# Block-causal attention feeding two mixture layers on one core: small two-operand VectorE steps turned into one-operand steps or handed to GpSimd, and the background squares tied to a place in ScalarE's queue

## The chip, the core and the metric

The program runs on one core of a Trainium2 chip. The metric is the device time of one execution in microseconds (us). The kernel before took 702.68 us as the median of three runs (700.4 to 709.11 us). Five engines work side by side: TensorE (PE, with its weight loads listed as PEld), VectorE (DVE), ScalarE (ACT), GpSimd (POOL) and the queue of SyncE (SP), which here only issues DMAs. Each engine takes its own instructions in the order fixed when the program was built, and waits at the head of its queue for what the instruction needs.

## What is computed

```
attention: 8 batches x 8 heads, 576 positions, head size 64, fp32
  scores = q k^T / 8, causal in blocks of 64 positions
  x = softmax(scores) v        -> 4608 tokens x 512
soft mixture: logits = x @ phi (32 slots)
  d = softmax over tokens, slot_in = d^T x, 8 experts (relu(slot_in w1) w2)
  c = softmax over slots, x = c @ slot_out
gated layer: (x w1) * (x w2) @ w3 @ w_out
```

The weights come as 64-bit floats and are narrowed to 32 bits on the chip with integer steps.

## The kernel before

The work goes in **pairs of heads**: 32 pairs, four to a batch. For a pair, PE computes raw scores only to find a row maximum per 64-block (`max_tile`, L177, seven tiles, each followed by a VectorE reduction into `bm`, L191 or L196). `level2` (L212) adds a mask to `bm`, once for each of five window lengths (L218, 250 elements per partition), and reduces to the row maxima `m` (L220). `mrow` (L223) turns `m` into rows through PE (L231, L234) that ScalarE copies into the operand set of the pair (L235). `qk_unit` (L241) then computes the scores again, transposed and with maximum and mask folded in, and ScalarE takes the exponentials into `PTa` (L263) and `PTb` (L271). `preadd` (L273) is GpSimd's: it adds pieces of the exponentials for the row sums (L287). `pv` (L297) multiplies by v, with the last 64 keys on half of the array's rows (L319). `sums` (L324) makes the row sums (L333). `prep_lo` (L148) splits the operands of a later pair on GpSimd (L153), and SP moves the parts into place (L174).

After each batch a **tail** of 18 steps (`push_tail`, L346) computes slot logits, the combine weights (`combine` to `combine3`, L394 to L407), the running maximum and sum of the dispatch softmax (`disp_max`, L432 to L458) and the sum over tokens (`slot_in`, L468, whose last 64 tokens use half the array's rows, L473). Its steps are spread over the following four pairs. The order inside a pair is one string, `ORDER` (L524), where M is a max tile, Q a score unit, T a tail step, L2 `level2`, MR `mrow`, A `preadd`, SU `sums`, V `pv`, PH and PL the operand preparation, LD the loads of the next operands.

BG in `ORDER` is one **background** turn: a DMA loads a piece of a weight of the last layer (L637) and `narrow` (L613) converts it: three integer steps on VectorE (L623, L624, L625), a square on ScalarE (L627) that marks values to be flushed, and a select on VectorE (L631). There are 16 pieces, spread over the pairs; one buffer holds the raw piece. `issue_after(ins)` puts an instruction behind `ins` in the queue of `ins`'s engine and binds no other engine: before, a turn's VectorE steps stand behind the `level2` of pair n+1 (L593), and its square on ScalarE is free. The program order is a priority only; a planner with a simulated timeline fixes each engine's order from it.

The later stage (`Rest.run`, L657 and `final`, L949) computes the experts and the last layer after the attention; the change does not touch it, but for the weights that the background turns have narrowed.

Of the kernel before, what the change touches and what calls it, by code (L numbers as in the profile page):

```python
# [54 lines left out]
class Attn:  # L55


    def __init__(self, tc, ctx, io, nb, keep, after_scores=None, background=()):
# [19 lines left out]
        self.bm, self.m, self.PT, self.acc, self.l2 = {}, {}, {}, {}, {}  # L78
# [4 lines left out]
        self.lmask = self.const.tile([128, 5, 2, 25], F32, name="lmask")  # L83
# [24 lines left out]
    def constants2(self):  # L108
# [7 lines left out]
        nc.gpsimd.memset(self.dT[:, S:SP], 0.0)  # L116

# [59 lines left out]
    def max_tile(self, n, i):  # L177
# [3 lines left out]
        if n not in self.bm:  # L181
            self.bm[n] = self.st_p.tile([128, 2, 25], F32, tag="bm", name="bm")
        bm, R1, T1 = self.bm[n], self.R1b[n % NB], self.T1b[n % NB]
# [9 lines left out]
        if i == 6:  # L193
            mm(0, 0, 4, 320, 256)
            mm(256, 1, 4, 576, 256)
            nc.vector.tensor_reduce(bm[:, :, 21:25], ps.rearrange("p (h n k) -> p h n k", h=2, k=64), axis=AX.X, op=ALU.max)  # L196
            return
        h, w = divmod(i, 3)
        k0 = KB[h]
        if w == 0:  # L200
            mm(0, h, 3, k0, 448)
            mm(448, h, 0, k0, 64)
            red(bm[:, h, 0:8], 512)
        elif w == 1:
            mm(0, h, 2, k0, 320)
            mm(320, h, 1, k0, 192)
            red(bm[:, h, 8:16], 512)
        else:
            mm(0, h, 4, k0 + 192 * h, 320)
            red(bm[:, h, 16:21], 320)  # L210

    def level2(self, n):  # L212
        if n not in self.bm or n >= self.n_pairs:
            return
        nc = self.nc
        bm = self.bm.pop(n)
        t = self.st_p.tile([128, 5, 2, 25], F32, tag="l2", name="l2")
        nc.vector.tensor_tensor(t, bm.unsqueeze(1).to_broadcast([128, 5, 2, 25]), self.lmask, op=ALU.add)  # L218
        m = self.st_p.tile([128, 5, 2], F32R, tag="m", name="m")
        self.l2[n] = nc.vector.tensor_reduce(m, t, axis=AX.X, op=ALU.max).ins  # L220
        self.m[n] = m

    def mrow(self, n):  # L223
# [7 lines left out]
        nc.tensor.matmul(a[0:2, 0:64], lhsT=m[:, 0, :], rhs=self.negI[:, 0:64], start=True, stop=True)  # L231
        for c in range(1, 5):
            o = a[0:2, 128 * c - 64:128 * c + 64] if c < 4 else b[0:2, 0:128]
            nc.tensor.matmul(o, lhsT=m[:, c, :], rhs=self.negI, start=True, stop=True)  # L234
# [6 lines left out]
    def qk_unit(self, n, h, u):  # L241
# [22 lines left out]
        else:  # L264
# [6 lines left out]
            nc.scalar.activation(out=PTb[:, S * h:S * h + w], in_=ps[:, 256:256 + w], func=AF.Exp, scale=SCALE)  # L271
# [25 lines left out]
    def pv(self, n, part):  # L297
# [48 lines left out]
    def push_tail(self, b):  # L346
# [10 lines left out]
        st = {}  # L357

# [43 lines left out]
        def combine3():  # L402
# [4 lines left out]
            nc.vector.tensor_tensor(C, C, sm.unsqueeze(2).to_broadcast([128, 5, 32]), op=ALU.mult)  # L407
# [24 lines left out]
        def disp_max():  # L432
# [4 lines left out]
            M, old = self.keep["M"][b % 2], self.keep["M"][1 - b % 2]  # L437
            mm = tl([128, 2], "dmm")
# [7 lines left out]
            ac = tl([128, 2], "dac")  # L446
# [3 lines left out]
            if b:  # L450
                al = tl([128, 1], "dal")
                nc.scalar.activation(out=al, in_=old, func=AF.Exp, bias=ng)
                nc.vector.tensor_tensor(Ls, Ls, al, op=ALU.mult)
                nc.vector.tensor_tensor(Ls, Ls, ac[:, 0:1], op=ALU.add)
                st["al"] = al
            else:
                nc.vector.tensor_copy(Ls, ac[:, 0:1])
            nc.vector.tensor_tensor(Ls, Ls, ac[:, 1:2], op=ALU.add)  # L458
# [9 lines left out]
        def slot_in():  # L468
# [3 lines left out]
            for g in range(4):  # L472
                nc.tensor.matmul(ps[32 * g:32 * g + 32, 128 * g:128 * g + 128], lhsT=st["d"][0:64, 4, :], rhs=xT[0:64, g, 512:640], start=False, stop=True)  # L473
# [655 lines left out]
```

## Time and profile before

| | |
|---|---|
| median of the runs | 702.68 us |
| time of the profiled execution | 702.59 us |
| its span, first to last instruction | 700.8 us |
| mean granted TensorE clock | 0.966 of full |
| busy: PE / VectorE / ScalarE / GpSimd | 634.3 / 512.6 / 348.0 / 343.0 us |
| attention, about | 0 to 460 us |
| experts, last weights | 461 to 588 us |
| final products | 588 to 701 us |

The span is split into stretches by when the lines run. The busy time of PE counts modelled ends of pipelined matmuls, so that a busy PE is not PE at its peak. The granted clock of a stretch is a mean of two levels, 1.0 (2.4 GHz) and 0.5 (1.2 GHz). "Idle before, releaser" says what ended an engine's idle time.

### The profile page before, as it was taken

What the parts mean: (1) busy time and instruction counts of PE and PEld (TensorE: products, weight loads), DVE (VectorE), ACT (ScalarE), POOL (GpSimd) and SP (SyncE); (2) the same over time, 40 slices, a digit from 0 to 9 for tenths busy, and PEclk for the clock granted to TensorE, in tenths of its full rate; (3) what the DMA queues carried; (4) which work ended last, traced back from release to release, by engine and by line L of the source; (5) the groups of instructions that cost most, each with busy time, mean ns of one, the idle gap of its engine ahead of it and who ended that gap; (6) DMA issues with size and microseconds to landing.
All of it is one profiled execution on the core that took longest, in us unless ns stands there. A gap on an engine that the chain in (4) does not pass through costs nothing. (4 is left out here: it accounts for less than half of the span.)

```text
span 700.8 us, 11771 instructions
## 1 busy us (share of the span) xinstructions
PE 634.3 (91%) x4423; PEld 451.2 (64%) x4423; DVE 512.6 (73%) x877; ACT 348.0 (50%) x638; POOL 343.0 (49%) x266
## 2 busy tenths in 40 slices
PE   4779898989997979997999999777999998999997
PEld 2667675766675757565777775533665566888886
DVE  7778778878878778788689666699962699645460
ACT  6756554645654654564465553244442335444441
POOL 7747674754764656566467454033432432233220
PEclk9889999999999999998899999997999999999999
DMA  6588876676867566867476767999988112566642
GB/s 205 152 212 206 242 179 198 169 185 164 237 150 202 150 174 148 213 175 181 123 195 159 209 219 246 353 337 388 394 312 314 63 61 74 170 214 214 226 174 90
DMA packets 59640, 141.53 MB, mean 202 GB/s; under 512 B 5800, under 2 KB 23848, under 8 KB 59560
## 3 DMA queue, kind: packets, MB, share of 16 engines
q1 hardware_dynamic: 59404, 140.71, 67.3%
q8 instruction: 35, 0.57, 0.3%
q14 instruction: 21, 0.17, 0.1%
q10 hardware_dynamic: 180, 0.07, 0.0%
HBM read 96.52 MB, written 10.32 MB: 152 GB/s over the span
## 5 line engine op out<-in xcount | busy, mean ns | idle before, releaser
L254 PE MATMUL sc<-set 128*128 128x320 f32 (+4 forms) x704 | 134.9, 326 | 9.8 <-ACT PTb L271 8.9
L191 DVE TENSOR_REDUCE bm<-mx 128x8 f32<-128x512 f32 (+1 forms) x192 | 113.4, 616 | 18.0 <-PE mx L188 17.0
L254 PEld LDWEIGHTS sc<-set 128*128 128x128 f32 x704 | 103.7, 199 | 18.5 <-ACT PTb L271 11.3
L287 POOL TENSOR_TENSOR acc<-PTa 128x640 f32<-128x640 f32 x31 | 49.2, 1588 | 134.7 <-PE sum L333 134.7
L188 PE MATMUL mx<-set 128*128 128x320 f32 (+4 forms) x384 | 89.2, 336 | 22.8 <-DVE bm L191 15.5
L1014 PE MATMUL ops<-H,Ph 128*128 128x512 f32 x288 | 90.7, 395 | 3.3 <-ACT H L918 2.4
L188 PEld LDWEIGHTS mx<-set 128*128 128x128 f32 x384 | 66.8, 210 | 37.9 <-DVE bm L191 20.3
L153 POOL TENSOR_TENSOR set<-raw,set 128x1152 fp32r<-128x1152 f32 x29 | 76.7, 2644 | 19.1 <-ACT set L145 18.9
L321 ACT COPY xT<-pv 128x320 f32<-128x320 f32 x64 | 25.3, 399 | 115.8 <-PE pv L319 96.3
L314 PE MATMUL pv<-PTa,v 128*64 128x320 f32 (+2 forms) x512 | 71.6, 380 | 0.0
L989 POOL TENSOR_TENSOR Pl<-rot,Ph 128x384 fp32r<-128x384 f32 x24 | 30.3, 1282 | 75.8 <-ACT Ph L987 75.8
L287 POOL TENSOR_TENSOR acc<-acc,PTb 128x640 f32<-128x640 f32 (+1 forms) x62 | 65.7, 1059 | 2.7
L1014 PEld LDWEIGHTS ops<-H,Ph 128*128 128x128 f32 x288 | 54.3, 189 | 17.0 <-ACT H L918 2.9
L263 ACT ACTIVATE PTa<-sc 128x960 f32<-128x960 f32 x64 | 59.5, 976 | 0.5 <-PE sc L254 0.4
L1014 PE MATMUL ops<-H,Pl 128*128 128x512 f32 x144 | 56.9, 395 | 0.0
L710 PE MATMUL wps<-wo,w 128*128 128x512 f32 x192 | 51.4, 412 | 2.9 <-POOL wo L655 1.7
L314 PEld LDWEIGHTS pv<-PTa,v 128*64 128x64 f32 x512 | 34.5, 140 | 29.0 <-issue 6.4
L1017 ACT COPY o<-ops 128x512 f32<-128x512 f32 x36 | 21.1, 588 | 57.0 <-PE ops L1016 56.7
L710 PEld LDWEIGHTS wps<-wo,w 128*128 128x128 f32 x192 | 35.2, 192 | 20.4 <-issue 6.7
L271 ACT ACTIVATE PTb<-sc 128x704 f32<-128x704 f32 x64 | 44.0, 694 | 7.5 <-PE sc L254 7.5
L314 PE MATMUL pv<-PTb,v 128*64 128x320 f32 (+1 forms) x256 | 44.4, 420 | 0.0
L655 POOL TENSOR_TENSOR w<-f,w 128x512 fp32r<-128x512 f32 x16 | 20.6, 1294 | 30.1 <-ACT w L654 27.4
(203 smaller groups left out, 1196.1 us busy)
## 6 DMA issues: line engine op xcount, KB each, us to landing
set<-set SPq DMA_DIRECT2D x116, 288.0 KB, 3.2
win<-in_moe_w SPq DMA_DIRECT2D x16, 2048.0 KB
raw<-in_qk SPq DMA_DIRECT2D x31, 576.0 KB, 5.1
v<-in_v SPq DMA_DIRECT2D x32, 288.0 KB, 4.3
rot<-cs SPq DMA_DIRECT2D x48, 192.0 KB, 3.7
out<-o SPq DMA_DIRECT2D x11, 768.0 KB, 4.5
raw<-in_moe_w SPq DMA_DIRECT2D x16, 512.0 KB, 4.7
w3raw<-in_w3T SPq DMA_DIRECT2D x16, 512.0 KB, 12.3
```

The source lines that it names most:

```text
L153: nc.gpsimd.tensor_tensor(T1[:, 0:2 * S], self.raw.pop(n), flat(R1).bitcast(F32), op=ALU.subtract)
L188: nc.tensor.matmul(ps[:, o0:o0 + kn], lhsT=R1[:, h, q0:q0 + 128], rhs=T1[:, k0:k0 + kn], start=True, stop=True)
L191: red = lambda out, n: nc.vector.tensor_reduce(out, ps[:, 0:n].rearrange("p (n k) -> p n k", k=64), axis=AX.X, op=ALU.max)
L254: nc.tensor.matmul(ps[:, o0:o0 + qn * (qs.stop - qs.start)], lhsT=lt[:, k0:k0 + 128], rhs=rt[:, qs, q0:q0 + qn], start=st, stop=not st)
L263: nc.scalar.activation(out=PTa[:, h], in_=ps[:, 0:960], func=AF.Exp, scale=SCALE)
L271: nc.scalar.activation(out=PTb[:, S * h:S * h + w], in_=ps[:, 256:256 + w], func=AF.Exp, scale=SCALE)
L287: add = lambda o, a, b: eng.tensor_tensor(o, a, b, op=ALU.add)
L314: nc.tensor.matmul(ps[64 * h:64 * h + 64, q0 - lo:q1 - lo], lhsT=v[:, 128 * j + 64 * h:128 * j + 64 * h + 64], rhs=pt[:, h, o:o + q1 - q0] ...
L321: nc.scalar.copy(self.xTb[b % 2][:, p, lo:hi], ps[:, 0:hi - lo])
L710: nc.tensor.matmul(p, lhsT=a[:, o], rhs=b, start=c + i == 0, stop=c == 7 and i == 2)
L989: eng.tensor_tensor(Pl[:, k], p, Ph[:, k].bitcast(F32), op=ALU.subtract)
L1014: nc.tensor.matmul(ps, lhsT=a[:, k, r], rhs=b[:, k], start=n == 0, stop=False)
```

## The change

`level2` works on a new layout: `bm` holds five windows of nine places in two fixed, zeroed buffers, the mask is added once (90 elements per partition instead of 250), on GpSimd for all pairs but the first two, and VectorE reduces nine places at a time. In the tail, the subtraction and the product of the combine weights go to GpSimd (VectorE keeps them in the last batch). The running maximum and the running sum become one-operand reductions over three columns; the product for the sum goes to ScalarE. In `pv` and `slot_in` the half-row matmuls use all 128 rows, the other half being multiplied by zeros. The background turns are split: turn i narrows piece i and then issues the load of piece i+1, and whatever a turn issues on ScalarE stands behind the last exponential of the preceding pair.

```diff
+        self.bmb = [self.const.tile([128, 2, 45], F32, name=f"bm{i}") for i in range(2)]
+        for t in self.bmb:
+            nc.vector.memset(t, 0.0)
...
+        for t in self.xTb:
+            nc.gpsimd.memset(t[64:128, :, S:SP], 0.0)
...
-        nc.vector.tensor_tensor(t, bm.unsqueeze(1).to_broadcast([128, 5, 2, 25]), self.lmask, op=ALU.add)
-        m = self.st_p.tile([128, 5, 2], F32R, tag="m", name="m")
-        self.l2[n] = nc.vector.tensor_reduce(m, t, axis=AX.X, op=ALU.max).ins
+        t = self.st_p.tile([128, 2, 45], F32, tag="l2", name="l2")
+        (nc.vector if n < self.ML else nc.gpsimd).tensor_tensor(t, self.bmb[n % 2], self.lmask, op=ALU.add)
+        m = self.st_p.tile([128, 2, 5], F32R, tag="m", name="m")
+        self.l2[n] = nc.vector.tensor_reduce(m, t.rearrange("p h (w k) -> p h w k", k=9), axis=AX.X, op=ALU.max).ins
...
+            self.last_exp[n] = nc.scalar.activation(out=PTb[:, S * h:S * h + w], in_=ps[:, 256:256 + w], func=AF.Exp, scale=SCALE).ins
...
-                r = slice(64 * h, 64 * h + 64)
-                nc.tensor.matmul(ps[r, 256:320], lhsT=v[r, 512:576], rhs=PTb[r, 2 * S + 64 * h:2 * S + 64 * h + 64],
+                nc.tensor.matmul(ps[64 * h:64 * h + 64, 256:320], lhsT=v[:, 512:576], rhs=PTb[:, 2 * S + 64 * h:2 * S + 64 * h + 64],
                                  start=False, stop=True)
...
+        eng = nc.vector if b == self.nb - 1 else nc.gpsimd
-            nc.vector.tensor_tensor(C, L, mx.unsqueeze(2).to_broadcast([128, 5, 32]), op=ALU.subtract)
+            eng.tensor_tensor(C, L, mx.unsqueeze(2).to_broadcast([128, 5, 32]), op=ALU.subtract)
-            nc.vector.tensor_tensor(C, C, sm.unsqueeze(2).to_broadcast([128, 5, 32]), op=ALU.mult)
+            eng.tensor_tensor(C, C, sm.unsqueeze(2).to_broadcast([128, 5, 32]), op=ALU.mult)
...
-            if b:
-                nc.vector.tensor_tensor(mm[:, 0:1], mm[:, 0:1], old, op=ALU.max)
-            nc.vector.tensor_tensor(M, mm[:, 0:1], mm[:, 1:2], op=ALU.max)
+            nc.vector.tensor_reduce(M, mm[:, 0:3 if b else 2], axis=AX.X, op=ALU.max)
...
-                nc.vector.tensor_tensor(Ls, Ls, al, op=ALU.mult)
-                nc.vector.tensor_tensor(Ls, Ls, ac[:, 0:1], op=ALU.add)
+                nc.scalar.mul(ac[:, 2:3], Ls, al)
-            nc.vector.tensor_tensor(Ls, Ls, ac[:, 1:2], op=ALU.add)
+            nc.vector.tensor_reduce(Ls, ac[:, 0:3 if b else 2], axis=AX.X, op=ALU.add)
...
-                nc.tensor.matmul(ps[32 * g:32 * g + 32, 128 * g:128 * g + 128], lhsT=st["d"][0:64, 4, :], rhs=xT[0:64, g, 512:640], start=False, stop=True)
+                nc.tensor.matmul(ps[32 * g:32 * g + 32, 128 * g:128 * g + 128], lhsT=st["d"][:, 4, :], rhs=xT[:, g, 512:640], start=False, stop=True)
...
-                    if self.background and n >= 2 and (BGP == 0 or n * 16 // BGP > (n - 1) * 16 // BGP):
-                        with self.tc.issue_after(self.l2[n + 1]) if n < BGF else nullcontext():
+                    if self.background and n >= 1 and (n == 1 or n * 16 // BGP > (n - 1) * 16 // BGP):
+                        with self.tc.issue_after(self.l2[n + 1]) if n < BGF else nullcontext(), self.tc.issue_after(self.last_exp[n - 1]):
                             self.background.popleft()()
...
+        def turn(i):
+            if i >= 0:
+                w, src, dc, f = pieces[i]
+                self.narrow(w[:, dc, f:f + 512], raws.pop(i), self.cv)
+            load(i + 1)
+        return [lambda i=i: turn(i) for i in range(-1, len(pieces))]
```

## Rows read from the trace of the kernel before

**Rows 1.** Stretches: us, busy by engine (instructions), PE clock, DMA share, GB/s
```profile
100.00:200.00 100.00, 92.19 (x746) 65.38 (x745) 82.57 (x148) 52.44 (x98) 60.02 (x44) 0.97 0.71 187
200.00:300.00 100.00, 88.93 (x722) 65.37 (x714) 80.92 (x146) 53.45 (x98) 59.89 (x45) 0.97 0.69 174
300.00:400.00 100.00, 94.32 (x755) 67.64 (x757) 81.58 (x150) 51.63 (x98) 58.75 (x46) 0.95 0.67 175
```
**Rows 2.** Waits of PE from 31 to 446 us: total us, times, longest
```profile
PE mx L188 <- DVE bm L191: 10.3, 7, 4.1
PE sc L254 <- ACT PTb L271: 8.4, 6, 4.1
PE mra L231 <- DVE m L220: 3.6, 1, 3.6
PE mx L188 <- DVE Sb L343: 2.3, 2, 1.7
```
**Rows 3.** Timeline, VectorE: last max reduction of three pairs, first column its start
```profile
74.08 0.68 DVE L196 TENSOR_REDUCE bm<-mx 128x8 f32<-128x512 f32 x1
...
348.29 0.68 DVE L196 TENSOR_REDUCE bm<-mx 128x8 f32<-128x512 f32 x1
...
395.31 0.68 DVE L196 TENSOR_REDUCE bm<-mx 128x8 f32<-128x512 f32 x1
```
**Rows 4.** Timeline around 218 us: start, us, instruction, idle before
```profile
216.22 1.27 DVE L442 TENSOR_TENSOR dmm<-dmm,M 128x1 f32<-128x1 f32 x1
217.44 2.60 POOL L153 TENSOR_TENSOR set<-raw,set 128x1152 fp32r<-128x1152 f32 x1
217.53 2.53 DVE L443 TENSOR_TENSOR M<-dmm 128x1 f32<-128x1 f32 x1
...
220.71 0.61 PE L188 MATMUL mx<-set 128*128 128x320 f32 x1 [4.10 <-DVE bm L191]
```
**Rows 5.** Timeline, 252 to 262 us: a piece's load, its square, PE behind it
```profile
252.65 0.79 SPq L637 DMA_DIRECT2D raw<-in_moe_w  x1
...
260.42 0.65 ACT L627 ACTIVATE m<-raw 128x512 bf16<-128x512 f32 x1 [4.52 <-DMA raw<-in_moe_w]
...
261.77 0.64 PE L254 MATMUL sc<-set 128*128 128x320 f32 x1 [4.14 <-ACT PTb L271]
```
**Rows 6.** Single lines: duration in ns, least/median/most, first and last start
```profile
L218 DVE TENSOR_TENSOR l<-bm,lmask x32: 398/596/2707, 17.8 to 407.2; 128x250 f32<-128x250 f32 x32
L407 DVE TENSOR_TENSOR c<-c,csm x7: 309/1454/2211, 113.1 to 420.4; 128x160 f32<-128x160 f32 x7
L443 DVE TENSOR_TENSOR M<-dmm x8: 158/1103/2528, 110.7 to 449.3; 128x1 f32<-128x1 f32 x8
L458 DVE TENSOR_TENSOR Ls<-Ls,dac x8: 149/159/2545, 115.9 to 452.0; 128x1 f32<-128x1 f32 x8
L625 DVE SCALAR_TENSOR_TENSOR u<-raw,u x16: 680/692/1904, 48.6 to 363.1; 128x512 int32<-128x512 int32 x16
```
**Rows 7.** Groups by line and shape: count, busy us, mean ns, idle before
```profile
L287 POOL TENSOR_TENSOR acc<-PTa 128x640 f32<-128x640 f32 x31 | 49.2, 1588 | 134.7 <-PE sum L333 134.7
L287 POOL TENSOR_TENSOR acc<-acc,PTb 128x128 f32<-128x128 f32 x31 | 16.3, 525 | 0.8
L452 ACT ACTIVATE dal<-M,dng 128x1 f32<-128x1 f32 x7 | 2.0, 287 | 0.0
L440 DVE TENSOR_REDUCE dmm<-LTb 128x1 f32<-128x64 f32 x8 | 1.7, 210 | 0.0
L319 PEld LDWEIGHTS pv<-PTb,v 64*64 64x64 f32 x128 | 6.2, 131 | 8.9 <-issue 8.9
L473 PEld LDWEIGHTS S<-xT,d 64*32 64x32 f32 x64 | 1.2, 104 | 6.2 <-issue 6.2
```
**Rows 8.** Waits of ScalarE and SP: total us, times, longest
```profile
ACT m L627 <- DMA raw<-in_moe_w: 20.7, 8, 4.5
SPq L637 <- DVE u L625: 10.1, 7, 1.9
```

More of the change, by code (lines that the diff above doesn't have):

```diff
@@ L82, in __init__ @@
         self.negI = self.const.tile([128, 128], F32R, name="negI")
-        self.lmask = self.const.tile([128, 5, 2, 25], F32, name="lmask")
+        self.lmask = self.const.tile([128, 2, 45], F32, name="lmask")
+        self.bmb = [self.const.tile([128, 2, 45], F32, name=f"bm{i}") for i in range(2)]
+        for t in self.bmb:
+            nc.vector.memset(t, 0.0)
         self.ones = self.const.tile([128, NP_B, 32], F32, name="ones")
@@ L180, in max_tile @@
         nc = self.nc
-        if n not in self.bm:
-            self.bm[n] = self.st_p.tile([128, 2, 25], F32, tag="bm", name="bm")
-        bm, R1, T1 = self.bm[n], self.R1b[n % NB], self.T1b[n % NB]
+        bm, R1, T1 = self.bmb[n % 2], self.R1b[n % NB], self.T1b[n % NB]
         ps = self.mx_p.tile([128, 512], F32, tag="pv", name="mx")
@@ L230, in mrow @@
         b = self.mx_p.tile([128, 512], F32, tag="pv", name="mrb")
[L231 removed]
+        nc.tensor.matmul(a[0:2, 0:64], lhsT=m[:, :, self.WIN[0]], rhs=self.negI[:, 0:64], start=True, stop=True)
         for c in range(1, 5):
             o = a[0:2, 128 * c - 64:128 * c + 64] if c < 4 else b[0:2, 0:128]
[L234 removed]
+            nc.tensor.matmul(o, lhsT=m[:, :, self.WIN[c]], rhs=self.negI, start=True, stop=True)
         nc.scalar.copy(R2[0:2, :, 0:448], a[0:2, 0:448].unsqueeze(1).to_broadcast([2, 2, 448]))
@@ L634, in background, with load @@
     def background(self):
-        def piece(w, src, dc, f):
-            raw = self.cv.tile([128, 1024], I32, tag="raw", name="raw64")
-            self.nc.sync.dma_start(out=raw, in_=self.io[src][128 * dc:128 * dc + 128, 2 * f:2 * f + 1024])
-            self.narrow(w[:, dc, f:f + 512], raw, self.cv)
-        return [lambda w=w, src=src, dc=dc, f=f: piece(w, src, dc, f) for w, src in ((self.wA, "moe2_w1"), (self.wB, "moe2_w2"))
-                for dc in range(4) for f in range(0, 1024, 512)]
+        pieces = [(w, src, dc, f) for w, src in ((self.wA, "moe2_w1"), (self.wB, "moe2_w2"))
+                  for dc in range(4) for f in range(0, 1024, 512)]
+        raws = {}
+        def load(i):
+            if i < len(pieces):
+                w, src, dc, f = pieces[i]
+                raws[i] = self.cv.tile([128, 1024], I32, tag="raw", name="raw64")
+                self.nc.sync.dma_start(out=raws[i], in_=self.io[src][128 * dc:128 * dc + 128, 2 * f:2 * f + 1024])
+        def turn(i):
+            if i >= 0:
+                w, src, dc, f = pieces[i]
+                self.narrow(w[:, dc, f:f + 512], raws.pop(i), self.cv)
+            load(i + 1)
+        return [lambda i=i: turn(i) for i in range(-1, len(pieces))]
     def load_expert(self, i):
@@ L1037, in setup @@
     keep["zeros"] = kp.tile([128, 512], mybir.dt.bfloat16, name="zeros")
-    keep["M"] = [kp.tile([128, 1], F32, name=f"M{i}") for i in range(2)]
+    keep["M"] = [kp.tile([128, 3], F32, name=f"M{i}") for i in range(2)]
     keep["Ls"] = kp.tile([128, 1], F32, name="Ls")
@@ L1087, in layout @@
         phib[64 * h:64 * h + 64, :, 32 * h:32 * h + 32] = ph[:, h].transpose(1, 0, 2)
-    lm = np.full((128, 5, 2, 25), -1e30, f)
-    for c, o, n in ((0, 7, 1), (1, 13, 3), (2, 8, 5), (3, 0, 7), (4, 16, 9)):
-        lm[:, c, :, o:o + n] = 0
+    lm = np.full((128, 2, 45), -1e30, f)
+    for c, o, n in ((0, 9, 1), (1, 27, 3), (2, 22, 5), (3, 2, 7), (4, 36, 9)):
+        lm[:, :, o:o + n] = 0
         if c:
             for h in range(2):
-                lm[:64, c, h, 21 if c == 4 and h else o + n - 1] = -1e30
+                lm[:64, h, 41 if c == 4 and h else o + n - 1] = -1e30
     rt = np.zeros((8, 2, 2 * S), f)
```

24 lines of the change are left out of this document (10 added, 14 removed).

## The prediction, made before the changed kernel was built or run

> **What bounds the kernel now.** I began with the chain of waits that ended last. It reaches back only to 461 us, and behind that it is the experts and the final products, which the change leaves alone. So the question is how early the attention hands over, and the table of stretches is the next view. In three stretches of 100 us PE is busy for 92, 89 and 94 us, and VectorE, the next, for about 81 [rows 1]. PE sets the pace, but with holes, and the granted clock has a mean of 0.97, 0.97 and 0.95: at a low level of half speed that is 3 + 3 + 5 = 11 us of PE work lost to slow stretches.
>
> The waits of PE name the holes [rows 2]. 10.3 us in seven waits are for a max reduction on VectorE, 8.4 us are for the exponential `PTb` on ScalarE, 2.3 us for the sums' step L343. The 3.6 us before L231 is one wait, at the start of the loop.
>
> Then the timeline, to see what stands ahead of the late engine. Around 218 us VectorE takes 1.27 us and then 2.53 us for steps on one element per partition (L442, L443). The second starts 0.09 us after GpSimd has begun a two-input step of 2.60 us and ends with it; behind it the max reductions are late, and PE idles for 4.10 us [rows 4]. The single lines show the same spread: L443 takes 158 ns at best and 2,528 at most, L407 309 and 2,211, L218 398 and 2,707, L458 149 and 2,545 [rows 6]. A VectorE step with two operands in SBUF waits out a GpSimd step that has started first. Nearly all of the 10.3 us lies behind L443, L442 or L407 in the tail of a batch.
>
> The other kind of hole: at 252.65 us SP issues a piece's load, the square stands in ScalarE's queue for 4.52 us until the data are there, the exponential behind it is late, and PE idles for 4.14 us [rows 5]. In all, ScalarE waits 20.7 us at the squares' head [rows 8].
>
> How much could go? The last max reductions of two pairs that lie five batches apart start at 74.08 and 348.29 us, 54.8 us a batch; the next batch, with one background piece left in it and no long hole, takes 47.0 us [rows 3]. Five times the difference is 39 us. That is a ceiling for what the holes and their clock cost.
>
> **The change part by part.** The profiled execution took 702.59 us, 0.09 under the median of the runs (702.68), so one sum serves both.
>
> *Small steps of the tail.* L442 and L443 become one reduction, L453, L454 and L458 another. The nearest row is a reduction of 64 elements, 210 ns [rows 7], and it has one operand, so it has nothing to wait out. L407 and L397 leave VectorE. The VectorE queue then no longer stands still there, and the max reductions behind follow at once. Of the 10.3 us [rows 2] I count 10. The bounds are 0, if other steps take over the waiting, and 10.3. What is late next is the sums' step behind L625, which keeps two operands and its 1,904 ns at most [rows 6]; the 2.3 us of PE's wait for L343 stay.
>
> *`level2`.* Its addition goes to GpSimd in 30 pairs. By the row of 128 elements, 525 ns [rows 7], 90 elements should lie between nothing and 525 ns; I take 0.45 us, in all 13.5 us of GpSimd. The two combine steps have 160 elements: scaled from the same row 0.65 us, in 14 steps 9 us. GpSimd is busy for about 60 us in 100 [rows 1] and stands waiting for PE's sums for 134.7 us [rows 7], so this is covered; if that cover goes, it becomes the third rival below. VectorE loses a step with a median of 596 ns a pair [rows 6]. Since PE has no wait for `m` after the first one of the loop [rows 2], the way over GpSimd has room, and the saved VectorE time has no direct price: I count 0 for it, with the same bounds as the wait, −3.6 to +3.6 us.
>
> The Trainium skill speaks against this part: its page "GPSIMD Engine Reference", section "3.1 Elementwise — side-by-side cycle accounting", has GpSimd 1.96 times slower than VectorE in a two-input addition and says to keep elementwise work on VectorE. No row here has the same addition on both engines; by its ratio the moved step would double, and the sum would not move as long as nobody waits for it.
>
> *Squares.* Each square now stands behind the last exponential of the preceding pair, so it can no longer be put far ahead of its data. The load does not come much earlier: there is one raw buffer, and SP already waits 10.1 us in seven places for L625 to release it [rows 8]. Of PE's 8.4 us behind `PTb` I count 8; the bounds are 0 and 8.4. SP's waiting stays as it is, since the load already stands behind L625.
>
> *Clock.* The low stretches follow the long holes. I remove 18 of the 21 us of holes in the loop (10.3 + 8.4 + 2.3) [rows 2], so of the 11 us I take the same share, 9.5. Bounds 0 and 11.
>
> *Full-row matmuls.* Before L319 the weight loads stand for 8.9 us with nothing to wait for, before L473 for 6.2 us [rows 7]: PE changes from full rows to half rows. Without that change both could go, 15.1 us at most. But in part that time only lets the preceding matmul finish, and a full-row tile loads as many rows again. Between 0 and 15.1 I take 4, nearer to the lower end.
>
> *New work.* ScalarE gets a product per batch but the first, like L452 at 287 ns: 7 × 0.287 = 2.0 us [rows 7], beside an engine half idle. The memsets at the start are four. I count 2 us against the change for both; bounds 0 and 2.
>
> Sum: 10 + 8 + 9.5 + 4 − 2 = 29.5 us, so 702.6 − 29.5 = **673 us**. The experts' stage starts earlier by that and keeps its length. With every upper bound, that is the 39 us of the batches and 15 us of the full rows, it is 649 us.
>
> **The rivals.** *The waiting stays and changes places.* GpSimd's new steps and its long ones still meet L624, L625 and L631, which keep two operands, and a step that was short may now be the one that meets them. Then the 10 us and their share of the clock, 9.5 × 10/18 = 5.3 us, stay, and 702.6 − (29.5 − 15.3) = 688 us comes out. For it: L625 reaches 1,904 ns, its median is 692 [rows 6]. Against it: its stalls are few, and the seven long waits of PE have shorter steps ahead of them. The Trainium skill's page "SBUF — State Buffer", section "Who interferes with whom", has the same rule: a VectorE step with two SBUF inputs and a GpSimd step that reads SBUF exclude each other, and whoever comes second waits for the whole of the other. The trace agrees: 2.53 us of waiting under a step of 2.60 us [rows 4].
>
> *The change doesn't do what it says.* The planner makes all orders anew from its simulated times, as it did when it put squares ahead of their data. A square has a lower limit only, and where turns follow in successive pairs the load is no earlier. If the holes reappear elsewhere, only the full rows remain: 702.6 − 4, say 698 us.
>
> *A new wait on GpSimd, slower.* If `level2`'s addition is put in GpSimd's queue behind the first addition of `preadd`, it waits with that for PE's sums and then for its 1,588 ns [rows 7]. `mrow`'s matmuls stand not far behind those sums on PE, so PE would wait some 1.59 + 0.45 us in each of 28 pairs, 57 us, and the result is 702.6 − 29.5 + 57 = 730 us. It decides the sign from about 1 us a pair. For it: GpSimd's queue stands at that addition for 134.7 us. Against it: `level2` comes ahead of `mrow` by the order, and in the planner's picture too its addition is ready while GpSimd idles.
>
> **How the numbers follow.** The forecast gets 0.66, with a range of its own from 655 to 688 us; waiting that changes places 0.16, the change without effect 0.12, the new wait 0.06. A measurement of this kernel can tell about 2%, 14 us, from no change: faster is below 688.6, slower above 716.7. Faster: 0.66 and half of the second case, 0.74. Slower: 0.06. Within: 0.20. The range from 652 to 696 us takes in the forecast's upper bounds nearly to their end, the second case and a part of the third; what it leaves out is about 0.2.
>
> **What would show it.** L443's successor at about 0.15 to 0.2 us in every batch, and no wait of PE for a max reduction above 2 us: the first term. No wait of ScalarE for `raw`, and PE's waits for `PTb` below 1 us: the second. A granted clock of 0.99 in the same stretches: the third. No idle time before L319's loads: the fourth. A batch of 47 us or less in the whole loop would hold them together. I would be wrong if PE waits for `m` before L231 in many pairs, if ScalarE waits for the combine weights from GpSimd, or if L625 and L631 become longer than now.

## The result, and the profile after

The changed kernel takes **670.28 us** (median of four runs, 667.67 to 673.66), beside 701.63 us for the kernel before in the same job: a ratio of 0.954 [0.947, 0.961]. The profiled execution has a span of 669.3 us against 700.8. The forecast was 673 us, in a range from 652 to 696. One execution among the runs below, of the kernel with the tail undone, took 769.46 us at a granted clock of 0.749 and is left out of that kernel's numbers.

The stretches come first, as in [rows 1] (us, busy by engine, PE clock, DMA share, GB/s). The last is the five batches between the first two marks of [rows 3], as found in this kernel.

```profile
100.00:200.00 100.00, 97.62 (x827) 72.51 (x826) 77.42 (x150) 59.17 (x108) 72.78 (x64) 1.00 0.76 200
200.00:300.00 100.00, 95.81 (x828) 71.83 (x825) 78.53 (x150) 62.19 (x115) 72.04 (x64) 1.00 0.78 208
78.90:315.90 237.00, 229.59 (x1960) 171.26 (x1960) 181.52 (x350) 145.16 (x266) 172.47 (x151) 1.00 0.77 204
```

PE is busy for 98 and 96 us in a hundred instead of 92 and 89, and the granted clock is at its upper level. The same five batches in the kernel before:

```profile
74.00:348.30 274.30, 247.75 (x1969) 178.26 (x1969) 219.96 (x393) 145.43 (x264) 164.62 (x123) 0.96 0.69 180
```

The five batches took 274.3 us and take 237.0. PE's idle time fell from 274.3 − 247.75 = 26.6 us to 237.0 − 229.59 = 7.4 us, which is 19.1 us. Its busy time fell by 18.2 us: a mean clock of 0.96 means 0.04 × 274 = 11 us of work lost to slow stretches before, and about 7 us remain by this estimate. The matmuls that became cheaper explain some 4 of them, as the experiments on the full rows show. The marks (last max reductions of the 7th, the 27th and the last pair, start and us):

```profile
78.86 0.67 DVE L199 TENSOR_REDUCE bm<-mx 128x8 f32<-128x512 f32 x1
...
315.86 0.68 DVE L199 TENSOR_REDUCE bm<-mx 128x8 f32<-128x512 f32 x1
...
373.49 0.69 DVE L199 TENSOR_REDUCE bm<-mx 128x8 f32<-128x512 f32 x1 [0.81 <-PE mx L191]
```

Beside [rows 3] the first mark comes 4.8 us **later**, the second 32.4 us earlier; the last pair stood at 405.91 us before. From it to the end it is 295.8 us against 294.9. So the loop gave 37.2 us, the filling of the pipeline took 4.8 back, the rest 0.9: 31.5 us, the difference of the spans.

PE's three largest waits from 31 to 430 us (total us, times, longest), to be read beside [rows 2]:

```profile
PE mrb L239 <- DVE Sb L348: 5.0, 3, 1.7
PE mx L191 <- DVE bm L194: 3.5, 5, 1.0
PE sc L259 <- ACT PTa L268: 3.2, 3, 2.2
```

The 10.3 us for max reductions are 3.5 us, none above 1.0, and the 8.4 us for `PTb` are gone. The step that the prediction named as the next late one, the sums behind the unpacking with two operands (now L627), costs 5.0 us. It did not grow by much: beside the 2.3 us of [rows 2] the kernel before had a second line for the same sums, 4.4 us together.

```profile
PE mrb L234 <- DVE Sb L343: 2.1, 2, 1.1
```

The single lines of the changed kernel (least/median/most ns), beside [rows 6]:

```profile
L448 DVE TENSOR_REDUCE M<-M x8: 109/142/157, 111.6 to 416.1; 128x1 f32<-128x3 f32 x7, 128x1 f32<-128x2 f32 x1
L223 POOL TENSOR_TENSOR l<-bm,lmask x30: 371/376/399, 31.8 to 374.9; 128x90 f32<-128x90 f32 x30
L403 POOL TENSOR_TENSOR c<-L,cmx x7: 455/458/722, 104.9 to 385.6; 128x160 f32<-128x160 f32 x7
L458 ACT ACTIVATE dac<-Ls,dal x7: 278/294/297, 161.8 to 418.2; 128x1 f32<-128x1 f32 x7
L627 DVE SCALAR_TENSOR_TENSOR u<-raw,u x16: 681/694/2034, 48.4 to 331.1; 128x512 int32<-128x512 int32 x16
```

The successor of L443 never takes more than 157 ns where L443 took up to 2,528. The waits of VectorE and ScalarE show what the change added and what it left:

```profile
DVE m L225 <- POOL l L223: 28.2, 24, 3.2
...
ACT m L629 <- DMA raw<-in_moe_w: 8.5, 3, 4.1
```

VectorE now stands 28.2 us for GpSimd's addition, and PE waits for `m` nowhere between 31 and 430 us: PE does not feel this wait. ScalarE still stands for a piece's data, 8.5 us instead of 20.7 [rows 8].

### The profile page after: what moved, and what is told of

Read it like the earlier page. It is cut to its first block, busy times and chain, and to the rows that moved or that the text cites. A ratio compares the mean times of both kernels' runs of the same rounds, so it can differ in the third digit from the quotient of the medians.

```text
span 669.3 us, 11760 instructions
## 1 busy us (share of the span) xinstructions
PE 618.5 (92%) x4423; PEld 448.1 (67%) x4423; DVE 456.9 (68%) x813; ACT 349.0 (52%) x645; POOL 359.4 (54%) x312
## 5 line engine op out<-in xcount | busy, mean ns | idle before, releaser
L259 PE MATMUL sc<-set 128*128 128x320 f32 (+4 forms) x704 | 132.1, 320 | 4.3 <-ACT PTa L268 3.2
L259 PEld LDWEIGHTS sc<-set 128*128 128x128 f32 x704 | 101.3, 195 | 14.3 <-issue 5.6
L191 PE MATMUL mx<-set 128*128 128x320 f32 (+4 forms) x384 | 86.0, 327 | 12.3 <-DVE bm L194 7.3
L191 PEld LDWEIGHTS mx<-set 128*128 128x128 f32 x384 | 64.0, 202 | 24.3 <-DVE bm L194 11.9
L1002 POOL TENSOR_TENSOR Pl<-rot,Ph 128x384 fp32r<-128x384 f32 x24 | 28.7, 1215 | 78.7 <-ACT Ph L1000 78.7
L319 PE MATMUL pv<-PTa,v 128*64 128x320 f32 (+2 forms) x512 | 70.1, 373 | 0.0
L292 POOL TENSOR_TENSOR acc<-acc,PTb 128x640 f32<-128x640 f32 (+1 forms) x62 | 63.6, 1025 | 2.3
## 6 DMA issues: line engine op xcount, KB each, us to landing
w3raw<-in_w3T SPq DMA_DIRECT2D x16, 512.0 KB, 12.2
```

The source lines that it names most:

```text
L191: nc.tensor.matmul(ps[:, o0:o0 + kn], lhsT=R1[:, h, q0:q0 + 128], rhs=T1[:, k0:k0 + kn], start=True, stop=True)
L259: nc.tensor.matmul(ps[:, o0:o0 + qn * (qs.stop - qs.start)], lhsT=lt[:, k0:k0 + 128], rhs=rt[:, qs, q0:q0 + qn], start=st, stop=not st)
L292: add = lambda o, a, b: eng.tensor_tensor(o, a, b, op=ALU.add)
L319: nc.tensor.matmul(ps[64 * h:64 * h + 64, q0 - lo:q1 - lo], lhsT=v[:, 128 * j + 64 * h:128 * j + 64 * h + 64], rhs=pt[:, h, o:o + q1 - q0] ...
L1002: eng.tensor_tensor(Pl[:, k], p, Ph[:, k].bitcast(F32), op=ALU.subtract)
```

## The experiments

Twelve kernels, each timed in five rounds beside the kernel before (its medians were 703.45 to 704.60 us). "7th pair" and "20 pairs" are the marks above in the profiled execution; "PE idle" is what PE's busy time leaves of the 20 pairs, and "clock" the granted clock in them; "end" runs from the last pair's mark to the end of the span.

| kernel | median us | ratio to before | 7th pair | 20 pairs | PE idle | clock | end |
|---|---|---|---|---|---|---|---|
| before | 702.68 | 1 | 74.1 | 274.2 | 26.6 | 0.96 | 294.9 |
| changed, again | 669.56 | 0.9505 [0.9462, 0.9547] | 77.7 | 237.0 | 7.4 | 1.00 | 295.5 |
| changed, tail undone | 689.52 | 0.9792 [0.9737, 0.9847] | 75.6 | 256.8 | 17.0 | 0.96 | 295.6 |
| changed, squares undone | 670.30 | 0.9510 [0.9467, 0.9552] | 74.0 | 240.3 | 8.5 | 0.99 | 295.6 |
| changed, full rows undone | 679.53 | 0.9647 [0.9600, 0.9694] | 76.5 | 241.2 | 6.9 | 1.00 | 300.3 |
| changed, `level2` undone | 676.78 | 0.9590 [0.9549, 0.9631] | 74.0 | 245.8 | 9.4 | 0.97 | 296.0 |
| changed, squares and `level2` undone | 682.08 | 0.9680 [0.9647, 0.9713] | 73.0 | 258.2 | 18.5 | 0.95 | 294.2 |
| before, tail alone | 688.37 | 0.9755 [0.9712, 0.9797] | 74.5 | 256.9 | 13.1 | 0.97 | 297.4 |
| before, squares alone | 686.95 | 0.9753 [0.9703, 0.9803] | 73.4 | 254.4 | 13.9 | 0.97 | 297.1 |
| before, full rows alone | 698.10 | 0.9900 [0.9868, 0.9932] | 73.2 | 267.9 | 25.9 | 0.96 | 295.8 |
| before, `level2` alone | 696.54 | 0.9897 [0.9868, 0.9926] | 73.9 | 259.8 | 19.1 | 0.97 | 298.5 |
| changed, steps with a scalar operand | 670.72 | 0.9532 [0.9502, 0.9563] | 76.7 | 238.1 | 8.4 | 1.00 | 294.9 |
| changed, `level2` late on GpSimd | 679.49 | 0.9652 [0.9617, 0.9686] | 76.8 | 240.0 | 8.8 | 1.00 | 299.8 |

Most of the end part is code that no edit touches, and still it ranges from 294.2 to 300.3 us. So a few microseconds of a difference between two medians can lie there, and the 20 pairs are the better measure of a part.

**The changed kernel again**, as the measure for the others. 

> The changed kernel once more, as the base of this chip for the three runs beside it. Expected: its ratio to the kernel before as measured first, 0.954, that is 670 us; every theory expects the same.

It came out as expected.

**The tail's small steps back** to two operands on VectorE, the combine steps too; the rest as changed:

```diff
-            nc.vector.tensor_reduce(M, mm[:, 0:3 if b else 2], axis=AX.X, op=ALU.max)
+            if b:
+                nc.vector.tensor_tensor(mm[:, 0:1], mm[:, 0:1], old, op=ALU.max)
+            nc.vector.tensor_tensor(M, mm[:, 0:1], mm[:, 1:2], op=ALU.max)
```

> The changed kernel with the tail's small steps put back: running maximum, running sum and the combine weights as two-operand steps on VectorE; everything else stays changed. Theory (these steps wait out a GpSimd step that began first, the max reductions behind them come late and PE idles): the first term and its share of the clock come back, 10 + 5 = 15 us, so 685 us, with waits of PE for the max reduction of 2 us and more and single steps on one element of over 1 us. Rival (with one background turn and level2 out of VectorE's queue there is room enough, and PE doesn't notice): at most 3 us, 673 us, though the steps are long again.

689.52 − 669.56 = 20.0 us. The step's line, then PE's wait and the stretch of the 20 pairs:

```profile
L450 DVE TENSOR_TENSOR M<-dmm x8: 159/813/1981, 108.1 to 433.5; 128x1 f32<-128x1 f32 x8
```
```profile
PE mx L191 <- DVE bm L194: 10.3, 10, 3.2
```
```profile
75.50:332.30 256.80, 239.77 (x1962) 179.14 (x1961) 202.40 (x373) 144.12 (x262) 170.65 (x141) 0.96 0.72 190
```

A step of 159 ns takes up to 1,981, PE's wait for the max reductions is 10.3 us again, and the clock is back at 0.96. Against the changed kernel's repeat the 20 pairs have 9.6 us more of idle time, which is the forecast's 10, and 10.1 us more of busy time at the lower clock, where the forecast had 5.3.

**The tail alone on the kernel before,** with the sums' steps on ScalarE and the combine steps on GpSimd as in the change.

```diff
-            if b:
-                nc.vector.tensor_tensor(mm[:, 0:1], mm[:, 0:1], old, op=ALU.max)
-            nc.vector.tensor_tensor(M, mm[:, 0:1], mm[:, 1:2], op=ALU.max)
+            nc.vector.tensor_reduce(M, mm[:, 0:3 if b else 2], axis=AX.X, op=ALU.max)
```

> The kernel before with the tail's small steps alone changed (running maximum and sum by one-operand reductions, combine weights on GpSimd). Theory (these steps waiting out GpSimd are the largest part of the gain; putting them back into the changed kernel cost 21 us): 15 to 21 us less than before, a ratio of 0.970 to 0.979, that is 682 to 688 us, and no wait of PE for a max reduction above 2 us. Rival (they are only worth that much once level2 has left VectorE too): less than 8 us, a ratio above 0.988.

Its 2.45% of 704.6 are 17.3 us. PE's waits:

```profile
PE sc L254 <- ACT PTb L271: 8.6, 6, 3.9
...
PE mx L188 <- DVE bm L191: 1.8, 2, 1.2
```

One kind of hole goes, the other stays.

**The squares' turns back:** no limit behind the last exponential, a piece's load in its own turn.

```diff
-                        with self.tc.issue_after(self.l2[n + 1]) if n < BGF else nullcontext(), self.tc.issue_after(self.last_exp[n - 1]):
+                        with self.tc.issue_after(self.l2[n + 1]) if n < BGF else nullcontext():
```

> The changed kernel with the background turns as they were: load and conversion in one turn, squares free in ScalarE's queue; everything else stays changed. Theory (the planner puts squares ahead of their data, and the exponential behind them holds PE): 8 + 4 = 12 us come back, so 682 us, with waits of ScalarE for the raw piece of 15 to 25 us in all and waits of PE for PTb of 2 to 4 us. Rival (the holes behind the squares were a chance of that one order): within 3 us of the changed kernel.

No change: 670.30 us. As the rival had it, ScalarE stands far longer for the data and PE hardly feels it; the timeline (start, us) shows what stands behind a late square:

```profile
ACT m L629 <- DMA raw<-in_moe_w: 30.3, 13, 5.5
```
```profile
181.82 0.66 ACT L629 ACTIVATE m<-raw 128x512 bf16<-128x512 f32 x1 [3.38 <-DMA raw<-in_moe_w]
182.39 0.38 ACT L382 COPY Lg<-lg 128x288 f32<-128x288 f32 x1
...
182.83 1.68 PE L380 MATMUL lg<-xT,phib 128*64 128x288 f32 x12 [0.38 <-ACT Lg L382]
```

Behind the 3.38 us of waiting is a copy for which PE waits 0.38 us. In this kernel no square stands directly ahead of a `PTb` exponential; in [rows 5] and at two more places of the kernel before one did, and those three cost PE 2.1, 4.1 and 1.6 us of the 8.4. The marks show 3.3 us lost in the 20 pairs and 3.7 us won back by the seventh pair.

**The squares alone on the kernel before,** the limit and the load one turn ahead.

```diff
-                        with self.tc.issue_after(self.l2[n + 1]) if n < BGF else nullcontext():
+                        with self.tc.issue_after(self.l2[n + 1]) if n < BGF else nullcontext(), self.tc.issue_after(self.last_exp[n - 1]):
```

> The kernel before with the background turns alone changed (load one turn ahead, squares behind the last exponential of the preceding pair). Forecast's theory (squares ahead of their data hold the exponentials that PE waits for, 8.4 us in its waits for PTb, and the clock behind them): 12 us less, a ratio of 0.983. Rival (a wait on ScalarE costs PE only where the order puts an exponential that PE needs at once behind it, and a new order puts other work there; with 30 us of such waits the changed kernel was no slower): within 4 us of before, a ratio of 0.994 to 1.006.

686.95 us, 17.4 us less, and more than either theory had. The holes for `PTb` are gone, those of the tail stay:

```profile
PE mx L188 <- DVE bm L191: 10.0, 3, 4.1
...
PE sc L254 <- ACT PTb L271: 0.6, 3, 0.2
```

So the same edit is worth 17 us on one kernel and nothing on the other. Something else in the change had to do its work there.

**`level2`'s addition back** on VectorE, on 90 elements as in the change.

```diff
-        (nc.vector if n < self.ML else nc.gpsimd).tensor_tensor(t, self.bmb[n % 2], self.lmask, op=ALU.add)
+        nc.vector.tensor_tensor(t, self.bmb[n % 2], self.lmask, op=ALU.add)
```

> The changed kernel with level2's addition on VectorE for all pairs, in the new layout of 90 elements; everything else stays changed. Forecast's theory (the way over GpSimd is covered and has no price; on VectorE the step waits out GpSimd's long steps again, in some ten pairs by 1 to 2.5 us): 0 to 10 us more than the changed kernel, 670 to 680 us. Rival (VectorE now stands 28 us in 24 places waiting for GpSimd's result, which costs as much as the waiting it replaced): the same within 2 us or up to 5 us less, 665 to 671 us.

7.2 us slower by the medians and 6.0 by the ratios, where the prediction had counted 0. The step's line, and one of its long instances in the timeline beside GpSimd's:

```profile
L223 DVE TENSOR_TENSOR l<-bm,lmask x32: 231/624/2162, 15.9 to 377.2; 128x90 f32<-128x90 f32 x32
```
```profile
223.52 2.66 POOL L158 TENSOR_TENSOR set<-raw,set 128x1152 fp32r<-128x1152 f32 x1
...
225.38 0.91 DVE L223 TENSOR_TENSOR l<-bm,lmask 128x90 f32<-128x90 f32 x1
```

It ends with GpSimd's step (226.29 beside 226.18). But PE has no hole behind this instance, nor behind another long one in the 20 pairs. PE's idle time there is 1.8 us for a DMA and three times about 2.4 us in the tail of a batch. In the tail other VectorE steps wait for GpSimd ahead of the max reductions, the select L633 among them, as here:

```profile
201.76 1.52 DVE L633 SCALAR_TENSOR_TENSOR wB<-m,u 128x512 f32<-128x512 bf16 x1
...
206.01 0.55 PE L191 MATMUL mx<-set 128*128 128x320 f32 x1 [1.48 <-DVE bm L194]
207.15 0.64 PE L191 MATMUL mx<-set 128*128 128x320 f32 x1 [0.58 <-DVE bm L194]
```

The changed kernel has one wait of 1.67 us at each of these three places, and its clock stays at 1.00. Here it is at 0.50 behind them, from 206.5 to 212.5 us at the place shown. So of the 8.8 us by which the 20 pairs are longer, 2.0 are idle time and 6.8 are busy time at the lower clock:

```profile
73.95:319.73 245.78, 236.39 (x1967) 177.98 (x1966) 193.36 (x369) 144.72 (x267) 166.16 (x133) 0.97 0.75 199
```

That the step itself holds PE is thus not what the trace shows; moving it changes the order that the planner finds, and the holes with it. Why this order has them was not isolated.

**Squares and `level2` back together,** to see whether one covers for the other: the edits of the two kernels, this line of each.

```diff
-        (nc.vector if n < self.ML else nc.gpsimd).tensor_tensor(t, self.bmb[n % 2], self.lmask, op=ALU.add)
+        nc.vector.tensor_tensor(t, self.bmb[n % 2], self.lmask, op=ALU.add)
...
-                        with self.tc.issue_after(self.l2[n + 1]) if n < BGF else nullcontext(), self.tc.issue_after(self.last_exp[n - 1]):
+                        with self.tc.issue_after(self.l2[n + 1]) if n < BGF else nullcontext():
```

> The changed kernel with two parts put back together: the background turns as they were, and level2's addition on VectorE for all pairs (in the new layout). Put back alone, the first cost nothing and the second 7 us. Theory (a waiting square costs PE only where the order sets an exponential PTb right behind it; moving level2 to GpSimd changed the order so that none stood there, and so hid what the squares' part is worth): with both put back the squares stand before PTb again, PE waits for PTb by 5 us or more, and the time is 10 to 17 us over the kernel with level2 alone put back, 685 to 694 us. Rival (the squares are harmless in every order that has the new tail and the full rows): 677 us, as with level2 alone put back, and PE's wait for PTb below 1 us.

682.08 us. That is 5.3 us over the kernel with `level2` alone undone, where the theory had 10 to 17 and the rival none: neither time holds. But PE's wait for `PTb` is back as the theory said, and with it a square just ahead of the exponential:

```profile
PE sc L259 <- ACT PTb L276: 9.1, 6, 5.1
```
```profile
252.91 0.66 ACT L629 ACTIVATE m<-raw 128x512 bf16<-128x512 f32 x1 [5.48 <-DMA raw<-in_moe_w]
253.47 0.74 ACT L276 ACTIVATE PTb<-sc 128x704 f32<-128x704 f32 x1
...
254.26 0.90 PE L259 MATMUL sc<-set 128*128 128x320 f32 x2 [5.09 <-ACT PTb L276]
```

This is the larger piece of what was missing. With the tail and the full rows done, the 20 pairs take 258.2 us; with the squares' part 245.8 (12.4 less), with `level2` on GpSimd 240.3 (17.9 less), with both 237.0 (21.2 less). The two overlap by 12.4 + 17.9 − 21.2 = 9.1 us. PE's idle time shows what they share: it falls from 18.5 to 9.4, to 8.5 and to 7.4 us, an overlap of 9.1 + 10.0 − 11.1 = 8.0 us, close to the 9.1 us of waits for `PTb`. In all four kernels with neither part (before, tail alone, full rows alone, and this one) three squares stand directly ahead of such an exponential; in those with either part none does. So the squares' part keeps them out of that place (its limit and its early load were not tested apart), and with `level2` on GpSimd the planner arrives at an order in which they do not stand there.

These are single executions. By the medians the overlap is smaller, 5.3 + 11.8 − 12.5 = 4.6 us. Nor is it all: the squares' part alone shortens the 20 pairs of the kernel before by 19.8 us and here by 12.4, and which part shares the remaining 7.4 was not tested.

**`level2` alone on the kernel before,** with its new layout.

```diff
-        nc.vector.tensor_tensor(t, bm.unsqueeze(1).to_broadcast([128, 5, 2, 25]), self.lmask, op=ALU.add)
+        (nc.vector if n < self.ML else nc.gpsimd).tensor_tensor(t, self.bmb[n % 2], self.lmask, op=ALU.add)
```

> The kernel before with level2 alone changed (new layout of 90 elements, addition on GpSimd from the third pair). Theory from the last run (the addition on GpSimd takes VectorE out of GpSimd's way in some ten pairs, worth about 6 us, and the new order keeps squares from standing ahead of PTb, worth 8 us of PE's waits and their clock): 15 to 20 us less than before, a ratio of 0.972 to 0.979, and PE's waits for PTb below 2 us. Rival (only its own 6 us): a ratio of 0.990 to 0.993, with the 8 us of waits for PTb still there.

696.54 us, 7.1 us less. The `PTb` holes are gone here too, as the theory said, but its 15 to 20 us did not come, and the tail's holes remain. The 20 pairs are 14.4 us shorter; the last five pairs then give back 2.1 us and the end 3.6.

```profile
PE mx L189 <- DVE bm L192: 11.6, 9, 4.8
PE mx L189 <- DVE dng L448: 3.2, 1, 3.2
```

**The full rows back** to half rows.

```diff
-                nc.tensor.matmul(ps[64 * h:64 * h + 64, 256:320], lhsT=v[:, 512:576], rhs=PTb[:, 2 * S + 64 * h:2 * S + 64 * h + 64],
+                nc.tensor.matmul(ps[r, 256:320], lhsT=v[r, 512:576], rhs=PTb[r, 2 * S + 64 * h:2 * S + 64 * h + 64],
...
-                nc.tensor.matmul(ps[32 * g:32 * g + 32, 128 * g:128 * g + 128], lhsT=st["d"][:, 4, :], rhs=xT[:, g, 512:640], start=False, stop=True)
+                nc.tensor.matmul(ps[32 * g:32 * g + 32, 128 * g:128 * g + 128], lhsT=st["d"][0:64, 4, :], rhs=xT[0:64, g, 512:640], start=False, stop=True)
```

> The changed kernel with the half-row matmuls of pv and slot_in put back; everything else stays changed. Theory (changing between full and half rows holds the weight loads): in the trace of the changed kernel the matmuls with the last 64 keys and the four before them take 0.44 us a pair against 0.68 before, 0.24 us in 32 pairs, so 4 to 8 us more than the changed kernel, 674 to 678 us. Rival (PE has that much slack in waits between the pairs, so the saved time becomes waiting): within 2 us.

10.0 us slower, of which 4.2 us lie in the 20 pairs and 4.8 us in the end part; the latter's cause was not isolated. The weight loads of the changed kernel (count, busy us, mean ns, idle before) beside [rows 7] tell which change of rows went away:

```profile
L324 PEld LDWEIGHTS pv<-PTb,v 128*64 128x64 f32 x128 | 9.2, 137 | 1.2
L475 PEld LDWEIGHTS S<-xT,d 128*32 128x32 f32 x64 | 2.2, 118 | 5.0 <-issue 4.9
```

The idle time before the loads of `pv` falls from 8.9 to 1.2 us; before those of `slot_in` it stays, 5.0 us after 6.2.

**Alone on the kernel before,** the two matmuls as in the change:

```diff
-                nc.tensor.matmul(ps[r, 256:320], lhsT=v[r, 512:576], rhs=PTb[r, 2 * S + 64 * h:2 * S + 64 * h + 64],
+                nc.tensor.matmul(ps[64 * h:64 * h + 64, 256:320], lhsT=v[:, 512:576], rhs=PTb[:, 2 * S + 64 * h:2 * S + 64 * h + 64],
```

> The kernel before with the full-row matmuls alone (pv's last 64 keys and slot_in's last 64 tokens). Theory (each change between full and half rows holds PE, and PE is the pace; putting them back cost 10 us): 7 to 10 us less than before, a ratio of 0.986 to 0.990, with 0.44 us instead of 0.68 us a pair for these matmuls and the four before. Rival (in the kernel before, with its holes, PE waits out the saved time): within 3 us.

7.0 us less (1.0% [0.7, 1.3] of 704.6), 6.3 of them in the 20 pairs. The price of a pair can be read in the timeline; first the kernel before, then the changed one (start, us, instruction):

```profile
185.86 0.49 PE L314 MATMUL pv<-PTa,v 128*64 128x192 f32 x4
186.28 0.33 PE L319 MATMUL pv<-PTb,v 64*64 64x64 f32 x4
186.54 0.65 PE L314 MATMUL pv<-PTb,v 128*64 128x256 f32 x4
```
```profile
47.34 0.49 PE L319 MATMUL pv<-PTa,v 128*64 128x192 f32 x4
47.67 0.28 PE L324 MATMUL pv<-PTb,v 128*64 128x64 f32 x4
47.78 0.60 PE L319 MATMUL pv<-PTb,v 128*64 128x256 f32 x4
```

From the start of the matmuls ahead to the start of those behind it is 0.68 us with half rows and 0.44 with full ones: 0.24 us. But this is the best case. In most pairs another operation stands behind, and there the same stretch takes 0.53 or 0.54 us, so that 0.15 are won. Over the 20 pairs the stretches add up to 13.8 us in the kernel with the full rows undone and to 10.0 us in the changed one: 3.7 us, or 0.19 us a pair, most of the 4.2 us measured, and less than the 0.24 us that the two expectations counted for every pair.

**Another form of the tail,** to ask whether the shape of the step matters or only its second tensor: five separate VectorE steps, each with one tensor and one scalar per partition, read from SBUF.

```diff
-            nc.vector.tensor_reduce(M, mm[:, 0:3 if b else 2], axis=AX.X, op=ALU.max)
+            if b:
+                nc.vector.tensor_scalar(mm[:, 0:1], mm[:, 0:1], old, None, op0=ALU.max)
+            nc.vector.tensor_scalar(M, mm[:, 0:1], mm[:, 1:2], None, op0=ALU.max)
```

> The changed kernel with the running maximum and sum again as five steps on VectorE, each with one tensor operand and the other as a scalar per partition, instead of two reductions; the combine weights stay on GpSimd. Theory (only a second tensor operand in SBUF makes VectorE wait out GpSimd; a scalar per partition doesn't): none of these steps above 0.3 us, and the time within 3 us of the changed kernel, 669 to 673 us. Rival (any second operand read from SBUF waits): steps of 1 to 2.5 us, and 680 to 690 us.

670.72 us, no different from the change.

```profile
L450 DVE TENSOR_SCALAR M<-dmm x8: 167/205/215, 109.5 to 414.6; 128x1 f32<-128x1 f32 x8
...
L460 DVE TENSOR_SCALAR Ls<-Ls,dal x7: 214/214/216, 157.7 to 416.4; 128x1 f32<-128x1 f32 x7
```

The same arithmetic with a second **tensor** took up to 1,981 ns; with a scalar it never exceeds 216, also when it starts under a long GpSimd step:

```profile
207.26 2.67 POOL L158 TENSOR_TENSOR set<-raw,set 128x1152 fp32r<-128x1152 f32 x1
...
207.78 0.21 DVE L460 TENSOR_SCALAR Ls<-Ls,dal 128x1 f32<-128x1 f32 x1
```

One tensor is not always enough, though. The changed kernel's L411 adds a constant to five elements per partition; in three batches it starts under a GpSimd step, takes 0.69 us and ends with it (205.05 beside 205.01):

```profile
L411 DVE TENSOR_SCALAR csm<-csm x8: 161/172/689, 109.2 to 423.1; 128x5 f32<-128x5 f32 x8
```
```profile
203.83 1.18 POOL L292 TENSOR_TENSOR acc<-PTb,PTa 128x256 f32<-128x256 f32 x1
...
204.36 0.69 DVE L411 TENSOR_SCALAR csm<-csm 128x5 f32<-128x5 f32 x1
```

The sums for which PE waits three times 1.67 us stand right behind it. One thing stays open: no run puts back the small steps without the combine steps. In the trace of the tail undone the five small steps take some 21 us more than at their least and the combine product 3.5, but how PE's 9.6 us divide between them was not tested.

**`level2` on VectorE for the first seven pairs** (the change has two), to win back the 4.8 us of the start.

```diff
-        (nc.vector if n < self.ML else nc.gpsimd).tensor_tensor(t, self.bmb[n % 2], self.lmask, op=ALU.add)
+        (nc.vector if n < 7 else nc.gpsimd).tensor_tensor(t, self.bmb[n % 2], self.lmask, op=ALU.add)
```

> The changed kernel with level2's addition on VectorE for the first seven pairs instead of two. In the changed kernel the seventh pair's last max reduction starts at 77.7 us; in the kernel with level2 on VectorE throughout it starts at 74.0 us, but later batches are longer there. Theory (in the filling of the pipeline GpSimd prepares the operand sets, and level2 behind it is late; later GpSimd has room): 3 to 4 us less than the changed kernel, 666 us. Rival (the early difference is given back in the first batch, since the operand sets set the pace): 669 to 671 us.

679.49 us, and neither theory holds. The seventh pair comes 0.9 us earlier than in the changed kernel's repeat, the 20 pairs take 3.0 us more, and the end part 4.3 us more. There PE stands idle among the experts, in a stretch in which it was full (first the changed kernel, then this one):

```profile
514.00:524.00 10.00, 10.00 (x68) 5.88 (x63) 6.23 (x13) 3.74 (x10) 6.00 (x6) 1.00 0.04 14
```
```profile
514.00:524.00 10.00, 7.18 (x44) 2.82 (x44) 3.85 (x8) 2.86 (x5) 4.42 (x4) 0.83 0.00 0
```

Why an edit at the start changes the experts' part 400 us later stays open. No kernel beat the changed one; squares undone and the scalar steps equal it.

## Why the prediction was right, and where its terms were not

**The total and its kinds held.** 29.5 us were forecast and 31.5 came in the profiled executions. Sorted by what PE lost, the 20 pairs gave 19.1 us of idle time (forecast 10 + 8 for the whole loop), by the estimate above 11 us of clock (9.5), and 7 us of other busy time (forecast 4, for the cheaper matmuls). The batch is 237.0 / 5 = 47.4 us; "47 us or less" was nearly met. What failed is that the prediction treated the parts as independent, and it left out the start. Undone one by one, the tail costs 20.0 us (15.3 with its clock), the squares 0.7 (12.2), `level2` 7.2 (0) and the full rows 10.0 (4): that the total was met to 2 us is in part luck, since misses of this size offset each other.

- **Small steps of the tail:** 10 us and 5.3 of clock were counted. Undone 20.0 us, alone 17.3. The mechanism is shown from both sides, by the step's line, PE's wait and the clock; the idle time was right (9.6 us) and the share of the clock too small (5.3 us beside 10.1 us of busy time). The Trainium skill's page "SBUF — State Buffer", section "Who interferes with whom", says that a VectorE step with at most one SBUF input does not contend with GpSimd, as long as it is outside the modes that use both ports. The reduction agrees, with 157 ns at most beside 1,981 for the same result from two tensors; L411, with one tensor and 689 ns, does wait, and no run here shows in which mode it ran.
- **Squares:** 8 us and 4.2 of clock. This step failed, as a term. The holes did close, but the change closes them twice. Alone the edit is worth 17.4 us; on top of the other parts it is worth nothing measurable (the ratios of the two are 0.9505 and 0.9510), because it gives 3.3 us in the 20 pairs and takes 3.7 at the start. The statement that ScalarE would not wait for `raw` was wrong as well, with 8.5 us in the changed kernel and 15.3 us in its repeat; what counts is what stands behind the square.
- **`level2`:** counted 0, worth 7.2 us undone. The bounds, −3.6 to +3.6, were taken from PE's one wait for `m`. But the price does not lie there, nor behind the step's own waiting of up to 2,162 ns: its place in the queues decides the order that the planner finds, and with it 2.0 us of holes and 6.8 us at the lower clock. The page "GPSIMD Engine Reference", section "3.1 Elementwise — side-by-side cycle accounting" of the Trainium skill would have kept the step on VectorE. The same addition takes 376 ns on GpSimd and 231 ns at best on VectorE, 1.63 times as long and not 1.96; yet following the rule costs 7.2 us here, with a median of 624 ns on VectorE.
- **Full rows:** 4 us, nearer to the lower end. Measured 4.2 us in the 20 pairs undone and 6.3 alone, 0.15 to 0.24 us a pair. The term was right in the loop and low for the whole kernel, where 10.0 us (undone) and 7.0 (alone) came out. Of the 15.1 us that "could go", `pv`'s part went, 8.9 to 1.2 us, and `slot_in`'s hardly, 6.2 to 5.0.
- **Clock:** 9.5 us of 11. It is 1.00 in the loop, so all 11 went. But the way of sharing it out failed: the prediction gave each hole its share by length. With the tail undone the clock is back at 0.96 though PE idles for 17.0 us and not 26.6. And with the squares undone one wait of 1.67 us (before 105.5 us) leaves it at 1.00, while behind one of 1.66 us (before 200.9 us) it is at 0.50 from 202.5 to 205.
- **New work:** −2. The product takes 294 ns (287 assumed) and nobody waits long for it. The real cost was not in the list: the pipeline fills 4.8 us later (3.7 in the repeat). Undoing either the squares' part or `level2` takes that away, doing either alone does not bring it, so it needs both; without the tail's part it is 1.5 us. By what path it comes was not settled.

**The rivals.** That the waiting changes places came true only in a corner: L627 still meets GpSimd with 2,034 ns at most, L411 behind it with 689, and the sums behind both cost PE 5.0 us, 0.6 more than before. That the planner's order could leave the squares without effect came true in a way not thought of: in the orders with `level2` on GpSimd the squares needed no limit. The new wait on GpSimd is there, 28.2 us long, but VectorE stands in it and PE does not.

## What to carry to other kernels

Price a hole once, and not once for each edit that removes it: before adding up the parts of a change, ask which holes they share, and test with one part undone, one part alone, and the suspected pair undone together. Of a waiting instruction the cost is what stands next in its queue: 30.3 us of ScalarE's waiting cost nothing measurable in one order, while three squares placed just ahead of an exponential that PE needed cost 8 us in another. Count a hole with the clock behind it, and read that from the trace: it did not follow the hole's length. Before a waiting step is blamed, look for the hole behind it; with `level2` back on VectorE its long waits had none. On VectorE, the small steps are the ones to take out of GpSimd's way, since a step of 0.15 us that waits for a long GpSimd step delays everything behind it; here one-element reductions and one-element steps with a per-partition scalar did not wait.

## What the runs showed of the hardware that was not expected

- A per-partition scalar read from SBUF did not make a one-element VectorE step wait for GpSimd: 216 ns at most in the lines shown, one of them under a GpSimd step of 2.67 us.
- A VectorE step with one tensor can wait for GpSimd all the same: L411, a constant added to five elements, takes 161 ns at best and 689 under a GpSimd step that began first.
- GpSimd takes 376 ns for the addition of 90 elements, with a spread of 371 to 399, and 458 ns for 160. In proportion to the 525 ns of the 128-element row this would be 369 and 656. The prediction took 450 and 650, so it was high on both, and the longer step costs less than that row suggests. Single steps of that row in the timeline take from 0.45 to 0.64 us.
- Four half-row matmuls between full-row ones cost 0.15 to 0.24 us a pair more than four full-row ones, though they load half the rows.
- A hole of the same length did not always cost clock: behind 1.67 us the granted clock stayed at 1.00, behind 1.66 us in the same execution (the squares undone) it then fell to 0.50 for some 2.5 us.
